# A two-layer attention and MLP kernel: planned instruction order, token-major q and k, a shifted MLP, and row-tiled remainders

## Chip, cores and metric

The kernel runs on one core of one Trainium2 chip. The metric is the device time of one execution in microseconds (us). Engines are called as in the profile: PE is the TensorE, PEld its weight loads, ACT the ScalarE, DVE the VectorE, POOL the GpSimd, SP the SyncE that issues most transfers. A bank is one of the slots of 512 columns that matmuls write to and that the other engines read.

## The reference

Two identical layers on 2048 tokens of width D = 576: windowed attention (32 heads of 18, each token sees the last 256), then an MLP of width 4608.

```python
def A(x, wqkv, wo):                       # H = 32, Dh = 18, W = 256
    q, k, v = split_heads(x @ wqkv)
    s = q @ k.T * Dh ** -0.5              # masked to 0 <= i - j < W
    return merge_heads(softmax(s) @ v) @ wo
def B(x, w1, b1, w2, b2):                 # F = 4608
    return gelu(layernorm(x) @ w1 + b1) @ w2 + b2
for _ in range(2):
    x = x + A(layernorm(x), wqkv, wo)
    x = x + B(layernorm(x), w1, b1, w2, b2)
```

## The kernel before

The tokens go through in chunks of 512 (four tiles of 128), eight chunks over the two layers. 576 is 4 x 128 + 64, so each contraction is five matmuls, the last with 64 rows of zeros. q and k are made head-major, with each head padded from 18 to 32 columns by scattered weights, so that four heads' scores run side by side as 32-row tiles:

```python
def qk_piece(k, g, which, ...):           # 8 groups of 4 heads; 16 pieces per chunk
    for c in range(KD):                   # KD = 5
        e.matmul(bank(bnk)[:, 0:CW], wpad[:, c, g*128:(g+1)*128], xnTa[:, c, :], ...)   # 512 columns
def scores(k, g, u):                      # one unit: writes all four score banks psS
    for (so, qo, nq, col) in parts:
        for j in range(4):
            e.matmul(psS[:, j, col:col+nq*128], kT[32*j:32*j+32, g, s, :], qT[32*j:32*j+32, g, ...],
                     tile_position=(32*j, 0))
    # then two exponentials on ACT (1024 columns each), selects on POOL for the mask
```

A chunk's attention has 8 x 3 such units. The order of instructions is written by hand. While chunk k is in its attention, the MLP of chunk k-1 is run between its parts (`...` marks cuts):

```python
for k in range(NK + 1):
    ...
    G_part(km, 0, ...)              # up projection and gelu, first half, of chunk k-1
    E_part(k, 0, base, byg)         # attention of chunk k, groups 0-3, beside down projection, first half
    G_part(km, 1, ...)              # up projection, second half
    E_part(k, 1, base, byg)         # attention, groups 4-7, beside down projection, second half
    for i in range(CT): att_T(i)    # transposes of the attention output
    ...
    for i in range(CT):             # the tail: nothing but v projections is left to lie beside it
        outproj(k, i, ...); ln_stats(ts[i]); ln_rstd(ts[i], True)
        ... ln_norm_T(ts[i - 1], xnTm, "xm")
```

The next up projection needs all of `xnTm`, so each chunk ends with a chain of output projection, norm and transposes through several engines.

The softmax here doesn't subtract the row's maximum and nothing guards it: scores larger than these inputs give would overflow.

## Time and profile before

| before | value |
|---|---|
| median of its runs beside the changed kernel | 1178.39 us (1175.69 to 1182.75, 4 runs) |
| span of the profiled run, granted clock | 1178.2 us, 0.961 |
| one steady chunk (272.46 to 414.85 us) | 142.39 us, PE busy 128.94 |
| before the first up projection | about 133 us, PE busy 70% of each of its two stages after the projections |

The page's first part gives each engine's busy time, its share of the span and its number of instructions:

```profile
PE 1028.5 (87%) x9312; PEld 580.0 (49%) x9312; DVE 306.8 (26%) x615; ACT 654.1 (56%) x927; POOL 353.2 (30%) x429
```

PE is the bound with 87%, and no other engine comes near. So time can be won in two ways: less work on PE, or fewer of the 150 us in which PE has none. The groups, the chain of waits, the stages and the timeline of before are shown and read in the prediction below.

### The profile page before, as it was taken

The page shows a single profiled execution, that of the slowest core. Times are in us where ns is not written, and L with a number is a line of the kernel's source. Part 1 is how long each engine was busy: PE and PEld are TensorE (multiplying, and loading weights), DVE is VectorE, ACT ScalarE, POOL GpSimd, SP SyncE. Part 2 cuts the span into 40 slices and gives each one's busy share as a digit, 9 for nine tenths or more (in the row PEclk, how much of TensorE's full clock was granted, in tenths as well). Part 3 has the DMA queues.
Part 4 walks back from the last instruction along what each step waited for, and adds up shares of the span by engine and source line. Part 5 has one row for each costly group of instructions (what it writes and reads, how often), then busy time and mean ns, then how long its engine had stood idle before and what let it go on. Part 6 is the DMA issues. An engine that isn't in the chain of part 4 may idle for free.

```text
span 1178.2 us, 22128 instructions
## 1 busy us (share of the span) xinstructions
PE 1028.5 (87%) x9312; PEld 580.0 (49%) x9312; DVE 306.8 (26%) x615; ACT 654.1 (56%) x927; POOL 353.2 (30%) x429
## 2 busy tenths in 40 slices
PE   3677799979999799898999899997998979898798
PEld 1233354544645445455545546454454644545366
DVE  8432312251213412034021521115020240102111
ACT  3364466646657276663656456573756627674432
POOL 9253132330414304151132314143040521424100
PEclk9897899999999899999999999999999989998899
DMA  9501414117230363306332171312633025331640
GB/s 242 155 2 23 85 41 140 54 34 205 70 103 22 71 169 91 101 2 147 92 112 81 29 191 61 112 51 50 199 92 101 17 52 169 93 105 35 179 130 21
DMA packets 158562, 109.78 MB, mean 93 GB/s; under 512 B 74176, under 2 KB 157760, under 8 KB 158464
## 3 DMA queue, kind: packets, MB, share of 16 engines
q1 hardware_dynamic: 151872, 105.41, 32.6%
q0 software_dynamic: 4768, 0.31, 0.8%
q10 hardware_dynamic: 1824, 2.65, 0.6%
q8 instruction: 73, 1.20, 0.4%
q14 instruction: 25, 0.20, 0.1%
HBM read 90.10 MB, written 2.36 MB: 78 GB/s over the span
## 4 chain that ended last, share of the span: by engine, by line
PE 73%; DVE 10%; ACT 8%; issue 5%; POOL 3%; DMA 1%; SPq 0%; POOLq 0%; DVEq 0%
PE ps L479 27%; PE ps L491 21%; PE ps L329 10%; ACT pT L396 5%; PE ps L426 5%; PE ps L388 5%; PE ps L356 4%; DVE st_all L280 3%; DVE x_res L454 3%; POOL pT L407 2%; DVE xn L299 2%; PE ps L464 1%; ACT hT L483 1%; ACT vA L365 1%; DVE mv_all L282 1%
## 5 line engine op out<-in xcount | busy, mean ns | idle before, releaser
L407 POOL TENSOR_SCALAR_AFFINE_SELECT pT<-pT 128x512 bf16<-128x512 bf16 (+1 forms) x368 | 277.4, 776 | 633.2 <-ACT pT L396 622.2
L396 ACT ACTIVATE pT<-ps 128x1024 bf16<-128x1024 f32 (+2 forms) x384 | 351.7, 967 | 168.7 <-PE ps L388 168.5
L479 PE MATMUL ps<-xnTm,w_sb 128*128 128x512 bf16 x1440 | 323.6, 387 | 6.0 <-DMA xnTm<-xn 6.0
L491 PE MATMUL ps<-w_sb,hT 128*128 128x288 bf16 x2304 | 317.5, 290 | 8.7 <-DVE x_res L454 8.1
L483 ACT ACTIVATE hT<-ps,b1col 128x512 bf16<-128x512 f32 x288 | 195.6, 687 | 138.9 <-PE ps L479 138.8
L491 PEld LDWEIGHTS ps<-w_sb,hT 128*128 128x128 bf16 x2304 | 218.6, 99 | 76.7 <-DVE x_res L454 11.3
L479 PEld LDWEIGHTS ps<-xnTm,w_sb 128*128 128x128 bf16 x1440 | 142.8, 100 | 180.8 <-issue 19.8
L454 DVE TENSOR_TENSOR x_res<-ps,x_res 128x576 f32<-128x576 f32 x80 | 60.0, 750 | 370.8 <-PE ps L491 321.9
L426 PE MATMUL ps<-vA,pT 128*128 128x20 bf16 x2880 | 102.8, 172 | 21.1 <-POOL pT L407 20.6
L426 PEld LDWEIGHTS ps<-vA,pT 128*128 128x128 bf16 x2880 | 85.7, 96 | 59.2 <-issue 41.6
L388 PE MATMUL ps<-qT,kT 32*128 32x384 bf16 (+2 forms) x1408 | 74.6, 279 | 37.2 <-ACT pT L396 25.5
L356 PE MATMUL ps<-wv_sb,xnTa 128*128 128x288 bf16 x320 | 58.6, 325 | 49.5 <-ACT vA L365 29.2
L329 PE MATMUL ps<-xnTa,wk_pad 128*128 128x512 bf16 x320 | 86.9, 406 | 16.3 <-DVE kT L335 6.3
L329 PE MATMUL ps<-xnTa,wq_pad 128*128 128x512 bf16 x320 | 84.7, 398 | 5.6 <-DVE kT L335 5.0
L335 DVE CAST qT<-ps 128x512 bf16<-128x512 f32 x49 | 33.8, 690 | 208.6 <-PE ps L329 208.4
L666 POOL TENSOR_TENSOR x_res<-x_res,b2bc 128x576 f32<-128x576 f32 x32 | 44.8, 1400 | 109.5 <-DVE xn L299 109.5
L388 PEld LDWEIGHTS ps<-qT,kT 32*128 32x128 bf16 x1408 | 22.3, 92 | 101.6 <-ACT pT L396 61.5
L356 PEld LDWEIGHTS ps<-wv_sb,xnTa 128*128 128x128 bf16 x320 | 31.5, 108 | 71.3 <-ACT vA L365 37.6
L365 ACT ACTIVATE vA<-ps 128x288 bf16<-128x288 f32 x64 | 26.1, 408 | 65.2 <-PE ps L356 65.2
L335 DVE CAST kT<-ps 128x256 bf16<-128x256 f32 (+1 forms) x78 | 40.4, 541 | 61.7 <-PE ps L329 61.7
L329 PEld LDWEIGHTS ps<-xnTa,wk_pad 128*128 128x128 bf16 x320 | 28.6, 102 | 54.5 <-ACT qT L337 9.4
L286 ACT ACTIVATE lnv<-mv_all 128x1 f32<-128x1 f32 x64 | 12.6, 197 | 68.7 <-DVE mv_all L282 68.7
(35 smaller groups left out, 383.9 us busy)
## 6 DMA issues: line engine op xcount, KB each, us to landing
w_sb<-in_B_w_dram SPq DMA_DIRECT2D x144, 288.0 KB, 4.6
w_sb<-in_B_w_dram SPq DMA_DIRECT2D x72, 512.0 KB, 4.0
w_sb<-in_B_w_dram SPq DMA_DIRECT2D x72, 64.0 KB, 3.8
hT<-in_A_x_dram SPq DMA_DIRECT2D x4, 576.0 KB, 10.8
out_dram<-xn SPq DMA_DIRECT2D x16, 144.0 KB, 1.8
w_sb<-in_A_wqkv_dram ACTq DMA_DIRECT2D x1, 1152.0 KB, 7.7
wv_sb<-in_A_wqkv_dram ACTq DMA_DIRECT2D x1, 576.0 KB, 10.5
wo_sb<-in_A_wo_dram ACTq DMA_DIRECT2D x1, 576.0 KB, 12.7
```

Of the source, the lines that this page charges most:

```text
L329: ins = e.matmul(bank(bnk)[:, 0:CW], wpad[:, c, g * 128:(g + 1) * 128], xnTa[:, c, :], start=(c == 0), stop=(c == KD - 1))
L335: S.add("dve", lambda e: e.tensor_copy(dst, src), reads=[f"pb{bnk}"], writes=wr)
L356: ins = e.matmul(bank(bnk)[:, 0:DHALF], xnTa[:, c, i * 128:(i + 1) * 128], wv_sb[:, c, hh * DHALF:(hh + 1) * DHALF], start=(c == 0), stop= ...
L388: ins = e.matmul(psS[:, j, col:col + nq * 128], kT[32 * j:32 * j + 32, g, s, :], qT[32 * j:32 * j + 32, g, qo * 128:(qo + nq) * 128], star ...
L396: S.add("act", lambda e, h2=h2: e.activation(pT[:, sl, 2 * h2:2 * h2 + 2, lo:hi], psS[:, 2 * h2:2 * h2 + 2, lo:hi], ACT.Exp, scale=SCALE), ...
L407: S.add("pool", lambda e, ap=ap, pat=pat, sgn=sgn, kind=kind: e.affine_select(ap, ap, pattern=pat, compare_op=(ALU.is_ge if kind == "d" el ...
L426: ins = e.matmul(bank(B_O)[:, o:o + VW], pT[:, sl, j, col + qi * 128:col + (qi + 1) * 128], vA[:, sv, 4 * g + j, :], start=(first and n == ...
L454: S.add("dve", lambda e: e.tensor_tensor(dst, src, xr, ALU.add), reads=[f"pb{b0}", f"pb{b0 + stp}", f"x{t}"], writes=[f"x{t}" if outp is N ...
L479: ins = e.matmul(bank(bnk)[:, 0:CW], w1_sb[:, sl, c, fo * 128:(fo + 1) * 128], xnTm[:, c, :], start=(c == 0), stop=(c == KD - 1))
L483: S.add("act", lambda e: e.activation(hT[:, fl, :], bank(bnk)[:, 0:CW], ACT.Gelu_apprx_tanh, bias=b1col[:, f:f + 1]), reads=[f"pb{bnk}", " ...
L491: ins = e.matmul(bank(bb[0] + hh * bb[1])[:, 0:DHALF], hT[:, fl, i * 128:(i + 1) * 128], w2_sb[:, fl, hh * DHALF:(hh + 1) * DHALF], start= ...
L666: S.add("pool", lambda e, t=t: e.tensor_tensor(x_res[:, t, :], x_res[:, t, :], b2bc[:, :], ALU.add), reads=[f"x{t}", "b2"], writes=[f"x{t}"])
```

## The change

Four things are done at once. q and k are computed token-major, unpadded, and brought to the head-major layout by a padded copy and DMA transposes. The two 64-row remainders of a pair of outputs run as two 64-row tiles side by side. The norm's inverse root moves from ACT to POOL. And the instructions are handed to a list scheduler (it places, one after the other, the instruction that can start earliest by the planned costs, the more urgent first), over a shifted order: the second half of a chunk's MLP lies one chunk later, so that a chunk's tail has an up-projection half beside it.

```diff
+    def two_out(lhs, rhs, n, reads, prio, after=()):      # a pair of outputs, q, k, v and output projection
+            for o in range(2):
+                for c in range(4):
+                    ins = e.matmul(bank(bs[o])[:, 0:n], lhs(o, c, full), rhs(o, c, full), start=(c == 0), stop=False)
+                if PAIR and o == 1:
+                    for oo in range(2):
+                        r = slice(64 * oo, 64 * oo + 64)
+                        ins = e.matmul(bank(bs[oo])[:, 0:n], lhs(oo, 4, r), rhs(oo, 4, r), start=False, stop=True,
+                                       tile_position=(64 * oo, 0))
...                                                        # the up projection has the same with 512 columns
+    def qkv(k, i, prio):                                  # one token tile
+        for n, w in enumerate("qkv"):
+            bs = two_out(... xnTa ..., ... wqkv ..., HB, ...)          # HB = 288 columns
...
+                    add("dve", ... e.tensor_copy(qv[:, o * 16:(o + 1) * 16, 0:DH], ...))   # qn, padded to 32 per head
+                add("sp", ... e.dma_start_transpose(dst, qn[:, sl, :]))                    # dst in qT or kT
...
+        add("pool", ... e.tensor_tensor(rstd[...], vtmp[...], nhalf[...], ALU.pow))
...
-    for k in range(NK + 1):                               # G_part, E_part, G_part, E_part, tail by hand
+    for k in range(NK + 1):                               # last number: priority in the list scheduler
+            E(k, range(0, 4), b - 0.5)                    # attention, groups 0-3, of chunk k
+            mm2(k - 2, 1, b)                              # down projection, second half, of chunk k-2
+            G_part(k - 1, 0, b + 1)                       # up projection, first half, of chunk k-1
+            E(k, range(4, 8), b + 1.5)                    # attention, groups 4-7
+            mm2(k - 1, 0, b + 2)                          # down projection, first half, of chunk k-1
+                    qkv(k + 1, i, b + 2.2 + 0.2 * i)
+            tail(k, b + 1.9)
+            G_part(k - 1, 1, b + 3)                       # up projection, second half: beside the tail of chunk k
+    PL.schedule()
```

Below, a cycle is this loop's body; its parts are called first attention half, first up half, second attention half and second up half.

## The prediction

> **What bounds the kernel now.** I read the page first, then the groups of instructions by line, the busy time by stage, the chain that ended last in order of time, and the timeline at single turns of the tensor engine. The page's chain of what ended last is by engine:
> ```profile
> PE 73%; DVE 10%; ACT 8%; issue 5%; POOL 3%; DMA 1%; SPq 0%; POOLq 0%; DVEq 0%
> ```
> So the TensorE (PE) is the bound, and the groups show what it does (busy us, mean ns of one, then idle time before them):
> ```profile
> L396 ACT ACTIVATE pT<-ps 128x1024 bf16<-128x1024 f32 (+2 forms) x384 | 351.7, 967 | 168.7 <-PE ps L388 168.5
> L479 PE MATMUL ps<-xnTm,w_sb 128*128 128x512 bf16 x1440 | 323.6, 387 | 6.0 <-DMA xnTm<-xn 6.0
> L491 PE MATMUL ps<-w_sb,hT 128*128 128x288 bf16 x2304 | 317.5, 290 | 8.7 <-DVE x_res L454 8.1
> L329 PE MATMUL ps<-xnTa,wk_pad 128*128 128x512 bf16 x320 | 86.9, 406 | 16.3 <-DVE kT L335 6.3
> L329 PE MATMUL ps<-xnTa,wq_pad 128*128 128x512 bf16 x320 | 84.7, 398 | 5.6 <-DVE kT L335 5.0
> L356 PE MATMUL ps<-wv_sb,xnTa 128*128 128x288 bf16 x320 | 58.6, 325 | 49.5 <-ACT vA L365 29.2
> ```
> The means there are latencies; matmuls overlap. The spacing comes from undisturbed blocks of the chain (start us, us):
> ```profile
> 1137.87 19.43 PE ps L479 x90
> 1157.30 17.65 PE ps L491 x144
> ```
> One 512-column matmul takes 19.43/90 = 0.216 us, one of 288 columns 17.65/144 = 0.1225 us. The stages are in the busy time by stretch (from:to, length, then PE, PEld, DVE, ACT, POOL busy, clock, DMA):
> ```profile
> 17.40:51.00 33.60, 27.70 (x120) 12.84 (x120) 22.35 (x50) 8.33 (x19) 14.28 (x21) 0.90 0.89 174
> 51.00:104.40 53.40, 37.53 (x488) 17.44 (x488) 17.77 (x40) 37.08 (x55) 28.24 (x40) 0.90 0.07 14
> 104.40:132.60 28.20, 19.82 (x93) 9.82 (x90) 10.59 (x22) 5.64 (x18) 5.59 (x4) 0.68 0.23 47
> 272.46:414.85 142.39, 128.94 (x1206) 73.00 (x1204) 37.34 (x74) 83.17 (x114) 42.42 (x52) 0.96 0.35 95
> 1097.70:1178.20 80.50, 77.21 (x468) 46.33 (x468) 6.06 (x8) 28.58 (x39) 0.00 (x0) 0.96 0.35 112
> ```
> They are: projections of chunk 0; attention of chunk 0, with no MLP beside it; its tail (output projection, norm, transposes); a steady chunk; the last MLP. A steady chunk has PE at 129 of 142 us, no other engine above 83. The first 133 us are slack, some of it at a clock of 0.68.
>
> Last, what a turn into row tiling and back costs. Timeline (start us, us):
> ```profile
> 157.30 2.38 PE L491 MATMUL ps<-w_sb,hT 128*128 128x288 bf16 x18
> 159.61 0.40 PE L388 MATMUL ps<-qT,kT 32*128 32x256 bf16 x8
> 159.94 0.56 PE L426 MATMUL ps<-vA,pT 128*128 128x20 bf16 x16
> ```
> The 18 full matmuls should take 18 x 0.1225 = 2.205 us, but the row-tiled scores start only after 2.31: 0.10 lost going in. The eight scores are two sets of four side by side, 2 x 256 columns, 2 x 0.11 = 0.22 us of streaming; the next full matmul starts after 0.33: 0.11 lost coming out. **One excursion costs about 0.2 us**, though none of these instructions shows a wait.
>
> **What the Trainium skill says.** "TensorEngine Tiling (Array Packing)", Tiling Modes, Key Properties: changing the tiling mode drains the TensorE, while tiles of one mode run in parallel. The trace agrees with both: 0.2 us per round trip above, and four scores taking the time of one. "TensorE: Matmul & The Clock Gate", Part 1: back-to-back matmuls are N/2.4 ns + about 2.5 ns apart (215.7 ns at 512); the trace has 216. Same part: the clock is halved until the engine has been busy for a window of about 3.4 us; the trace agrees in kind, with clock 0.68 in the gappy tail of chunk 0 against 0.96 to 1.0 in steady stretches. So filling gaps pays twice.
>
> **The change part by part**, in PE time.
> 1. q and k token-major. Before, heads padded from 18 to 32 columns make 640 matmuls of 512 columns, 640 x 0.216 = 138.2 us, and v has 320 x 0.1225 = 39.2: 177.4 us. Unpaired and token-major, q, k and v are 32 token tiles x 3 x 2 halves x 5 = 960 matmuls of 288: 117.6 us. **Saves 60 us.** It adds 64 DMA transposes of 128x1024, and moves v's 64 evictions (26.1 us) from ACT to DVE, which gets 192 of 288 columns, by ACT's 408 ns about 78 us, for the 74 us of q and k evictions it had: DVE about even, ACT 26 down.
> 2. Row-tiled remainders. A pair of outputs takes nine slots, not ten, plus an excursion. MLP up: 8 chunks x 18 pairs = 144, each -0.216 + 0.2 = -0.016 us: 2 saved. Projections: 96 for q, k, v and 32 for the output, each -0.1225 + 0.2 = +0.08: 10 lost. **Costs 8 us net**; streaming falls by 47 us but 272 excursions cost 54. I believe the turn costs the same with 64-row tiles as with 32-row ones; this is the least secure step.
> 3. Norm by POOL pow instead of Ln and Exp on ACT: 12.6 + 13.0 us off ACT, off the bound. It shortens a chain in the tail only if POOL isn't busy.
> 4. The shifted, list-scheduled order. The second half of the down projection of one chunk goes beside the attention of the chunk after next, so that the tail of each chunk and the transposes lie beside an up-projection half (90 matmuls, 19.4 us). This takes waits away, and is best summed by stage.
>
> One cycle's PE work after: up projection 36 pairs/2 = 18 x (9 x 0.216 + 0.2) = 38.6; down 288 x 0.1225 = 35.3; q, k, v 12 x (9 x 0.1225 + 0.2) = 15.6; output projection 4 x 1.3 = 5.2; scores 24 units x (0.22 + 0.2) = 10.1; PV 384 matmuls, which the timeline spaces by about 0.025 us (16 in 0.40), 9.6. Sum 114.4. Before by the same rates it is 38.9 + 35.3 + 22.2 + 4.9 + 10.1 + 9.6 = 121, against 140 measured (six steady chunks, 838 us): **19 us per chunk of waits and clock**. I expect 6 of these to stay, a judgement: the timeline shows PE waiting 0.5 to 0.9 us for ACT at each change between up projection and attention, four a cycle, and with three banks for projections and down projection some eviction waits can't be filled.
>
> By stage: first matmul at 14 (before 17.5: no scatter of padded weights, but the same load, norm and transpose). Projections of chunk 0: 12 x (1.3 + 0.6 waiting for one of three banks) = 23. Attention of chunk 0: bound by its exponentials, ACT busy 37 before, so 42 (before 53). First attention half of chunk 1 beside chunk 0's tail: 12 units x 1.95 of ACT, 25. Rest of chunk 1: 19.3 + 19.7 + 17.6 + 15.6 + 5.2 + 19.3 = 97, less about 10 done early in the ACT-bound stretch: 87. Six cycles: 6 x 114.4 - 5 (first chunk of layer 2 has three quarters of the blocks) - 15.6 (the last has no next projections) = 666, plus 6 x 6 waits = 702. End: three down halves of 17.65, two up halves of 19.3, and 4 to the output = 95.5, with 3 of waits 98. Sum 14 + 23 + 42 + 25 + 87 + 702 + 98 = 991; half clock in the opening gaps, an estimate from the 0.90 and 0.68 above, adds 14: **1005 us**, a ratio of 0.853. So of 174 us gained some 52 are arithmetic (parts 1 and 2) and some 120 are gaps.
>
> **Rivals.** (a) The 64-row turn is free: 54 us less, 951. For: the authors chose it. Against: the excursions above. (b) The transposes become the wait. Their issue is serial on one queue:
> ```profile
> 250.07 5.19 SPq L446 DMA_TRANSPOSE attT<-attq  x4
> ```
> That is 1.3 us for 640 columns, so an estimated 2.1 for 1024. After the attention of a chunk come 4 + 4 x 1.3 and 8 x 2.1 = 27 us before the next scores (q and k have one buffer). Against: 19.3 of up projection and some 10 to 20 of projections stand there to cover it. If 10 us per cycle stick out: 1075. (c) The fixed order is made from planned costs; where real ones differ (the excursions, issue on one queue) engines stand before a blocked instruction, and the 19 us per chunk return: 6 x 13 more, 1085. (d) ACT becomes the bound: 654 - 26 - 26 - 13 for q and k = 589 us, 59% of 1005, but near PE in attention halves (12 x 1.95 = 23 against 27). It doesn't bind except in chunks 0 and 1.
>
> **Range and chances.** (a) partly true gives 960 to 980, (b) or (c) partly 1040 to 1065: range 955 to 1065. To be within 2% all the gaps must stay and part 1 must be lost to transposes: 3%. Slower by over 2%: 1%.
>
> **What would show it.** Steady cycle near 120 us with PE near full; 288-column matmuls replacing L329; each 64-row pair starting 0.1 us late and its follower 0.1 us late, with no wait named; PE's idle time (span less busy, 150 us before) under 90; clock over 0.96. Wrong, if 64-row turns show no extra spacing, if scores wait for transposes of q or k in every cycle, or if the cycle stays over 130.

## The result

The changed kernel took 1046.28 us (median of 4 runs, 1041.77 to 1053.11) beside 1178.39. Ratios are the mean time of one kernel's fast runs over that of the other's of the same rounds, so not quite the ratio of the medians; here 0.8881, with a 95% interval of 0.8822 to 0.8939. The time lies in the range, 41 us above its centre. The profiled run has a span of 1046.7 us and a clock of 0.933, lower than before.

The page after, first part and chain by engine:

```profile
PE 954.4 (91%) x9312; PEld 537.5 (51%) x9312; DVE 331.3 (32%) x840; ACT 576.3 (55%) x705; POOL 380.8 (36%) x517
```

```profile
PE 75%; POOL 10%; issue 8%; ACT 3%; DMA 2%; DVE 2%; POOLq 0%; SPq 0%
```

PE has 74 us less to do and idles for 1046.7 - 954.4 = 92 us, not 150. POOL's share of the chain went from 3 to 10%, a first hint of where the rest is. The groups of matmuls after (busy us, mean ns, idle before and its releaser):

```profile
L680 PE MATMUL ps<-xnTm,w_sb 128*128 128x512 bf16 x1152 | 290.4, 394 | 6.4 <-ACT pT L563 6.4
L683 PE MATMUL ps<-xnTm,w_sb 64*128 64x512 bf16 x288 | 57.1, 394 | 0.0
L716 PE MATMUL ps<-w_sb,hT 128*128 128x288 bf16 x2304 | 312.7, 286 | 0.0
...
L485 PE MATMUL ps<-wqkv,xnTa 128*128 128x288 bf16 x768 | 129.2, 306 | 26.0 <-DMA xnTa<-xn 25.9
```

The 640 padded matmuls of 512 columns are gone; for q, k and v there are now 768 full ones of 288 columns and, on a line not shown, 192 of 64 rows. L683 is the 64-row pair of the up projection; no wait is named ahead of it. What it costs shows in the timeline of one stretch of up projection (start us, us):

```profile
164.78 1.90 PE L680 MATMUL ps<-xnTm,w_sb 128*128 128x512 bf16 x8
166.61 0.39 PE L683 MATMUL ps<-xnTm,w_sb 64*128 64x512 bf16 x2
166.93 1.90 PE L680 MATMUL ps<-xnTm,w_sb 128*128 128x512 bf16 x8
```

Eight full matmuls should take 8 x 0.216 = 1.73 us, but the pair starts after 1.83: 0.10 lost going in. The pair streams 0.216, but the next full one starts after 0.32: 0.10 lost coming out. In the raw starts of the trace the loss is 96 ns in and 103 ns out. A pair of 512 columns so takes 415 ns in place of 2 x 216 = 432, and one of 288 columns 321 ns in place of 245.

The busy time by stretch (from:to, length, then PE, PEld, DVE, ACT, POOL busy, clock, DMA):

```profile
16.78:35.54 18.76, 16.24 (x90) 8.04 (x91) 12.19 (x38) 0.00 (x0) 8.72 (x16) 0.91 1.32 188
35.54:103.92 68.38, 42.15 (x566) 23.96 (x567) 26.64 (x72) 36.29 (x48) 31.25 (x44) 0.72 0.48 113
103.92:147.50 43.58, 32.10 (x397) 17.80 (x398) 26.22 (x63) 22.55 (x24) 26.67 (x34) 0.77 0.29 57
...
589.80:712.00 122.20, 119.26 (x1206) 67.14 (x1205) 40.71 (x104) 74.42 (x88) 45.96 (x62) 0.96 0.48 117
...
832.90:953.20 120.30, 106.16 (x1087) 58.48 (x1085) 22.89 (x61) 74.48 (x90) 45.82 (x61) 0.89 0.39 108
```

The first three are the projections of chunk 0, its attention, and its tail beside the first attention half of chunk 1. The fourth is a full cycle: PE is busy 98% of it, in 122 us where a chunk took 142. The fifth is the last cycle: it has 119 PE instructions less than the one above and 13 us less PE work, yet takes almost as long. So the new time is lost in the opening and in the last cycle, and both have a low clock.

Against the prediction's stages, by bounds taken from the first up projection and from ACT's table loads:

| stage | predicted, us | measured, us |
|---|---|---|
| to the first matmul | 14 | 16.8 |
| projections of chunk 0 | 23 | 18.8 |
| attention of chunk 0 | 42 | 68.4 |
| chunk 0's tail beside the first half of chunk 1 | 25 | 43.6 |
| half clock in the opening | 14 | inside the lines above |
| rest of chunk 1 (to 234.9) | 87 | 87.4 |
| five cycles (to 832.9) | 5 x 120.4 - 5 = 597 | 598.0 |
| last cycle (to 953.2) | 120.4 - 15.6 = 104.8 | 120.3 |
| end | 98 | 93.5 |
| sum | 1005 | 1046.8 |

The opening is 29.5 us over, the last cycle 15.5, the end 4.5 under, the rest within 1.5.

### The profile page after: what moved, and what is told of

The parts are those of the page before. It is cut to its first block, busy times and chain, and to the rows that moved or that the text cites. A ratio compares the mean times of both kernels' runs of the same rounds, so it can differ in the third digit from the quotient of the medians.

```text
span 1046.7 us, 22452 instructions
## 1 busy us (share of the span) xinstructions
PE 954.4 (91%) x9312; PEld 537.5 (51%) x9312; DVE 331.3 (32%) x840; ACT 576.3 (55%) x705; POOL 380.8 (36%) x517
## 4 chain that ended last, share of the span: by engine, by line
PE 75%; POOL 10%; issue 8%; ACT 3%; DMA 2%; DVE 2%; POOLq 0%; SPq 0%
PE ps L716 27%; PE ps L680 27%; POOL pT L584 9%; PE ps L485 6%; PE ps L601 5%; PE ps L683 5%; PE ps L554 4%; ACT pT L563 3%; PE ps L489 1%; DMA xnTa<-xn 1%; DVE st_all L413 1%; DMA hT<-in_A_x_dram 1%; POOL rstd L426 0%; DMA qT<-qn 0%; POOL x_res L659 0%
## 5 line engine op out<-in xcount | busy, mean ns | idle before, releaser
L680 PE MATMUL ps<-xnTm,w_sb 128*128 128x512 bf16 x1152 | 290.4, 394 | 6.4 <-ACT pT L563 6.4
L680 PEld LDWEIGHTS ps<-xnTm,w_sb 128*128 128x128 bf16 x1152 | 102.1, 100 | 141.1 <-issue 35.4
L635 DVE TENSOR_TENSOR x_res<-ps,x_res 128x288 f32<-128x288 f32 x160 | 71.0, 452 | 317.3 <-PE ps L716 263.2
L485 PE MATMUL ps<-wqkv,xnTa 128*128 128x288 bf16 x768 | 129.2, 306 | 26.0 <-DMA xnTa<-xn 25.9
L485 PEld LDWEIGHTS ps<-wqkv,xnTa 128*128 128x128 bf16 x768 | 68.4, 102 | 58.8 <-issue 24.5
L521 DVE CAST qn<-ps 128x288 bf16<-128x288 f32 x128 | 52.7, 453 | 95.7 <-PE ps L489 95.7
L611 DVE RECIPROCAL rinv<-ps 128x16 f32<-128x16 f32 x64 | 16.4, 256 | 167.0 <-PE ps L601 167.0
L683 PE MATMUL ps<-xnTm,w_sb 64*128 64x512 bf16 x288 | 57.1, 394 | 0.0
L436 DVE TENSOR_SCALAR xn<-x_res,mv_all,rstd 128x576 bf16<-128x576 f32 x60 | 43.9, 732 | 22.9 <-POOL rstd L426 9.0
L683 PEld LDWEIGHTS ps<-xnTm,w_sb 64*128 64x128 bf16 x288 | 13.8, 93 | 63.5 <-issue 63.5
L413 DVE BATCH_NORM_STATS2 st_all<-x_res 128x6 f32<-128x288 f32 x96 | 41.4, 452 | 1.1
```

The source lines that it names most:

```text
L413: add("dve", lambda e, i=i, s=s: e.bn_stats(st_all[:, t, i, :], s[:, t, i * HB:(i + 1) * HB]), reads=res, writes=[f"st{t}_{i}"], cost=0.43 ...
L485: ins = e.matmul(bank(bs[o])[:, 0:n], lhs(o, c, full), rhs(o, c, full), start=(c == 0), stop=False)
L521: add("dve", lambda e, o=o, b=bs[o], qv=qv: e.tensor_copy(qv[:, o * 16:(o + 1) * 16, 0:DH], bank(b)[:, 0:HB].rearrange("p (h d) -> p h d", ...
L635: add("dve", lambda e: e.tensor_tensor(x_res[:, t, sl], bank(b)[:, 0:HB], x_res[:, t, sl], ALU.add), reads=[b], writes=[f"x{t}h{hh}"], cos ...
L680: ins = e.matmul(bank(bks[o])[:, 0:n], w1_sb[:, sl, col:col + 128], xnTm[:, k % 2, c, 0:n], start=(c == 0), stop=False)
L683: ins = e.matmul(bank(bks[oo])[:, 0:n], w1_sb[64 * oo:64 * oo + 64, sl, 2048 + pp * 128:2048 + (pp + 1) * 128], xnTm[64 * oo:64 * oo + 64, ...
```

## The experiments

Four kernels went to the chip in each of three batches, each with its own runs of the kernel before beside it (medians 1177.78, 1177.75 and 1178.67 us). The theory was that the turns into row tiling cost about what the tiling saves, that the shift and the plan give most of the gain, and that the opening's loss comes from scores and exponentials taking turns. The rivals were that turns are cheap, that transposes set the pace, and that the arithmetic of q and k gives the gain.

### after_again: the changed kernel unchanged

> The changed kernel as it is, timed once more beside its variants on one chip. Every theory: 1040 to 1053 us, as in its first four runs; it is the measure for the three runs beside it.

Measured: 1046.58 us (1042.74 to 1051.07), ratio 0.8887 [0.8859, 0.8914]. This is the value that the others are held against.

### e_nopair and e_pair_mlp: no pairs, and pairs in the up projection alone, with a new plan

```diff
-PAIR = True
-W1W = 2304
+PP = False      # projections
+PM = False      # up projection; True in e_pair_mlp, where W1W stays 2304
+W1W = 2560
 ...             # each use of PAIR becomes PP or PM; unpaired remainders are zero-padded to 128 rows
```

> No row-tiled pairs anywhere: remainder padded with zeros to 128 rows, as before the change. Turn theory (each pair loses 96 ns going in and about 103 ns coming out, read from the spacing in the changed kernel's trace): up projection 144 x (432 - 415) = +2.4 us, projections 128 x (245 - 321) = -9.8 us, so about 7 us faster than the changed kernel. Rival (a pair is worth the matmul that it saves): streaming grows by 144 x 0.216 + 128 x 0.1225 = 47 us, so 40 us or more slower.

Measured: 1034.12 us (1032.56 to 1036.31), ratio 0.8783 [0.8758, 0.8808].

> Pairs kept in the up projection alone; q, k, v and output projection padded. Turn theory: -9.8 us against the changed kernel, and 2 us under the kernel without any pair. Rival: 128 x 0.1225 = 16 us slower than the changed kernel.

Measured: 1047.38 us (1045.30 to 1051.23), ratio 0.8900 [0.8872, 0.8927].

Without pairs the kernel is 12 us faster, so they bring nothing here. But the two runs don't fit one theory: the pairs of the up projection should save 2 us and seem to cost 13. The scheduler makes a new plan for each set of costs, and the plans differ: in e_nopair the first up projection starts at 140.7 us, in the changed kernel at 148.2 by ACT's table load. So what was measured was partly the plan. The next two hold it fixed.

### e_plan_nopair and e_plan_mlp_full: the same plan, with the 64-row pairs replaced

```diff
                 if PAIR and o == 1:
                     for oo in range(2):
-                        r = slice(64 * oo, 64 * oo + 64)
-                        ins = e.matmul(bank(bs[oo])[:, 0:n], lhs(oo, 4, r), rhs(oo, 4, r), start=False, stop=True, tile_position=(64 * oo, 0))
+                        ins = e.matmul(bank(bs[oo])[:, 0:n], lhs(oo, 4, full), rhs(oo, 4, full), start=False, stop=True)
 ...             # planned costs unchanged; rows 64 to 127 of the last weight block are zeroed
```

In e_plan_mlp_full this is done in the up projection alone. The order of PE's instructions was compared and is the same as in the changed kernel. Not all else is: e_plan_nopair also drops four small weight loads at the start and adds three memsets.

> The changed kernel's plan kept to the letter (same tasks, same order on the tensor engine, same waits, same banks); only the two row-tiled matmuls of each pair are two full matmuls with zero-padded weights. This takes out what a new plan does. Turn theory: 144 x (432 - 415) = +2.4 us in the up projection and 128 x (245 - 321) = -9.8 us in the projections, so 5 to 10 us faster than the changed kernel (1036 to 1041). Rival (a pair saves what its streaming says): 35 to 47 us slower.

Measured: 1042.43 us (1036.39 to 1046.12), ratio 0.8845 [0.8813, 0.8877].

> Same plan again, pairs kept in the q, k, v and output projections, two full matmuls in their place in the up projection alone. Turn theory: the pair of 512 columns costs 96 + 216 + 103 = 415 ns against 432, so 0 to 3 us slower than the changed kernel, and 7 to 12 us slower than the run without any pair. The run of the pairs in the up projection alone (1047) asks whether a pair there costs some 10 us that the spacing doesn't show; if so, this run is 10 us faster than the changed kernel.

Measured: 1045.26 us (1041.74 to 1046.89), ratio 0.8877 [0.8850, 0.8904].

e_plan_nopair's timeline of the same kind of stretch (start us, us):

```profile
161.34 1.89 PE L682 MATMUL ps<-xnTm,w_sb 128*128 128x512 bf16 x8
163.07 0.59 PE L686 MATMUL ps<-xnTm,w_sb 128*128 128x512 bf16 x2
163.50 1.89 PE L682 MATMUL ps<-xnTm,w_sb 128*128 128x512 bf16 x8
```

Ten full matmuls take 163.50 - 161.34 = 2.16 us, and eight and a pair took 166.93 - 164.78 = 2.15. The first two lines show no loss between them: 1.73 us for eight. So in the up projection the pair is worth nothing. Taken from the spacings, all pairs save 144 x 17 ns = 2.4 us there and cost 128 x 76 ns = 9.7 us in the projections, 7.3 net. The whole-kernel times give 1046.6 x (0.8845/0.8887 - 1) = -4.9 us and -1.2 us; their intervals overlap with that of the changed kernel, so the sign of either isn't settled by them. Of the 4.9 us, 3.5 lie before the first up projection (144.7 us by ACT's table load, against 148.2), where the dropped loads may have a part. The rival, under which replacing the pairs would cost 47 us, is refuted.

### e_spread and e_spread2: spread the down projection over an attention half

```diff
+        if pace is not None:
+            order.add(pace)                               # in the list scheduler: not before this score unit
 ...
-            mm2(k - 2, 1, b)
+            mm2(k - 2, 1, b, [] if last else SC[-12:])    # pieces of 6 matmuls paced by the 12 score units
 ...                                                       # e_spread2: mm2(k - 1, 0, ...) too, the second half
```

> In the first attention half of each chunk, each group of six down-projection matmuls may only be placed once a matching score unit has been placed (two groups per unit, three groups ahead), so that the filler lasts to the end of the half. My theory of the attention halves: one unit can't be shorter than 2.44 us (scores, then two exponentials, one set of score banks), and the list scheduler puts 18 matmuls in each of the first eight units (3.04 us each) and none in the last four (about 2.5 us with the tensor engine idle); spread evenly 12 units take about 31 us where the half took 36, so about 5 us per chunk for six chunks: 25 to 30 us faster, idle time and half clock at the ends of the halves gone. Rival (the half is bound by the exponentials or by the select anyway): no change, within 5 us.

Measured: 1035.38 us (1032.96 to 1036.63), ratio 0.8788 [0.8764, 0.8813].

> The down projection paced by the score units in both attention halves. The run that paced the first half alone gained 11 us, not 25 to 30: its trace shows that I had the wrong half, the first is already full with the next chunk's projections, and the idle stretches at half clock (seen at 190 to 205, 313 to 330, 443 to 450 us) end the second halves, which have 36 us for 27 us of work. Theory: second halves go from 36 to about 31.5 us, seven of them, so 25 to 34 us below the changed kernel beyond the 11: 1003 to 1012. Rival (the exponentials and the select set the length of the half): 1035, as with the first half alone.

Measured: 1041.02 us (1039.08 to 1044.95), ratio 0.8838 [0.8811, 0.8865].

e_spread gains 11 us. e_spread2's 6 us aren't settled, as its interval overlaps with the changed kernel's. Both are far from what was expected. The stretches show why: first a second attention half, then the first one of the next cycle, of the changed kernel, then the same two of e_spread2.

```profile
291.40:327.70 36.30, 33.72 (x450) 22.09 (x448) 9.10 (x22) 24.54 (x25) 17.23 (x22) 0.92 0.35 94
357.10:392.80 35.70, 35.36 (x479) 23.69 (x478) 17.93 (x43) 24.51 (x26) 19.50 (x25) 1.00 0.47 117
```

```profile
286.30:321.90 35.60, 35.51 (x482) 24.14 (x480) 11.55 (x28) 24.50 (x26) 17.23 (x23) 1.00 0.21 45
350.30:388.40 38.10, 34.26 (x442) 22.83 (x443) 13.06 (x34) 24.58 (x26) 18.20 (x24) 0.87 0.55 140
```

The PE hole and the low clock moved from one half to the other. The filler, that is the work that can lie between the score units (down projection, projections, output projection), is short over the cycle as a whole: filling one half empties the other. By ACT's table loads e_spread2's cycles from 228.3 us are 121.9 and 123.2 us long, no shorter than the changed kernel's 122.2 and 120.9; its last one is, with 114.1 against 120.3. I had also named the wrong half for e_spread, for first halves were full already. My expectation of 25 us and more fell.

### e_open: weight loads after the transposes of the opening

```diff
-        w1_load(0, [f"q{n0 - 1}"])
-    w2_load(0, 0, [f"q{n0 - 1}"])
+        w1_load(0, [f"q{n0 - 1}"] + [f"xa{i}" for i in range(n0)])
+    w2_load(0, 0, [f"q{n0 - 1}"] + [f"xa{i}" for i in range(n0)])
```

> One thing changed in the opening: the 17 weight loads of the first MLP are issued after the four transposes of chunk 1's normed input, not before. Theory: in the changed kernel these loads stand ahead on the one issuing queue, the transposes land at 53, and the tensor engine, whose next instruction needs them, is idle from 46 to 53 us; so 6 to 9 us faster (1037 to 1041), all of it before 60 us. Rival (attention of chunk 0 is paced by its exponentials, and the hole is made up by 148 us): under 2 us.

Measured: 1044.58 us (1040.69 to 1046.27), ratio 0.8861 [0.8834, 0.8888]. The timeline of the changed kernel and then of e_open, at the start of chunk 1's projections (in brackets the idle time before and its releaser; SPq is the transfer queue's issue):

```profile
39.47 6.32 SPq L365 DMA_DIRECT2D w_sb<-in_B_w_dram  x9
...
45.90 7.34 SPq L445 DMA_TRANSPOSE xnTa<-xn  x4
...
52.90 1.14 PE L485 MATMUL ps<-wqkv,xnTa 128*128 128x288 bf16 x4 [6.95 <-DMA xnTa<-xn]
```

```profile
47.19 1.14 PE L485 MATMUL ps<-wqkv,xnTa 128*128 128x288 bf16 x4 [0.89 <-DMA xnTa<-xn]
```

The transposes stood behind weight loads in one queue, and the hole of 7 us on PE was theirs; ordered otherwise, it is gone. Yet the first up projection starts 2.8 us earlier only (145.4 against 148.2), and the total moves by about 3 us, within the intervals: later transposes of k then stand behind the weights. A hole at one place of a loose stretch is worth little.

### e_split: the scores of a unit as two halves, in the opening alone

```diff
+        cut = k == 0 or (k == 1 and g < 4)
+        for js in (((0, 1), (2, 3)) if cut else ((0, 1, 2, 3),)):
 ...
-        add("pe", fn, reads=rd, writes=[f"pb{j}" for j in range(4)], cost=0.06 + ncol * 0.00053, prio=prio, lat=0.15)
+            sc = add("pe", fn, reads=rd, writes=[f"pb{j}" for j in js], cost=0.06 + ncol * 0.00053, prio=prio, lat=0.15)
```

The first half of a unit's scores then needs only the two banks that the first exponential has read.

> In the attention stretches of the opening alone (chunk 0, first half of chunk 1: 36 units) the scores of a unit are two tasks of two heads each, so the next unit's first pair may run while the second exponential of this unit reads the other banks. Theory for the 44 us by which the opening missed my prediction: I took the exponentials' busy time as the pace, but one set of score banks makes each unit wait for scores and exponentials in turn (2.44 us where the exponentials take 1.94); so up to 36 x 0.5 = 18 us, 8 to 18 us faster, all before the first up projection, which starts near 135 and not 148. Rival (the pace of the opening is the select on POOL with the bias adds and transposes, or issue order): under 4 us.

Measured: 1033.35 us (1030.25 to 1034.22), ratio 0.8767 [0.8745, 0.8788], clock 0.944 to 0.950. The timeline of the changed kernel where PE has nothing else, then of e_split:

```profile
192.43 0.40 PE L554 MATMUL ps<-qT,kT 32*128 32x384 bf16 x8
192.88 1.94 ACT L563 ACTIVATE pT<-ps 128x1024 bf16<-128x1024 f32 x2 [0.51 <-PE ps L554]
194.88 0.40 PE L554 MATMUL ps<-qT,kT 32*128 32x256 bf16 x8
195.32 1.94 ACT L563 ACTIVATE pT<-ps 128x1024 bf16<-128x1024 f32 x2 [0.50 <-PE ps L554]
```

```profile
77.32 4.48 ACT L565 ACTIVATE pT<-ps 128x1024 bf16<-128x1024 f32 x6 [0.88 <-PE ps L558]
```

In the changed kernel all four score banks are written by one unit, so the next scores wait for both exponentials, and these for the scores: a unit takes 195.32 - 192.88 = 2.44 us, not the 1.94 of its exponentials. In the opening the changed kernel has the same gap, 0.5 to 0.7 us ahead of each unit's exponentials from 80 to 98 us. In e_split six exponentials follow each other without a gap. Attention of chunk 0 in e_split, by stretch:

```profile
34.00:93.10 59.10, 48.13 (x575) 25.87 (x573) 27.15 (x76) 36.28 (x48) 31.05 (x44) 0.79 0.58 132
```

It fell from 68.4 to 59.1 us, the first up projection starts at 133.6 us, and the kernel gains 13 us, inside what was expected. The plan is new here too, but the hole behind the weight loads is still there (5.25 us before 52.20), so the gain isn't that. This mechanism is confirmed.

### e_head: undo the token-major q and k alone

```diff
-    wqkv = sb("wqkv", [P, KD, 3 * D], BF16)
+    wv_sb = sb("wv_sb", [P, KD, D], BF16)
+    wq_pad = sb("wq_pad", [P, KD, G * 128], BF16)
+    wk_pad = sb("wk_pad", [P, KD, G * 128], BF16)
 ...
+    def qk(k, g, prio):                                   # 5 matmuls of 512 columns, as in the kernel before
+        for which, wpad in (("q", wq_pad), ("k", wk_pad)):
 ...                                                       # no qn, no transposes of q and k; shift, pairs and scheduler stay
```

> Undoes the token-major q and k alone: padded head-major projections (640 matmuls of 512 columns, straight into the tiles that the scores read, no transposes of q and k), v and everything else as in the changed kernel, planned anew. My step 1: 640 x 0.216 = 138.2 us against 64 pairs of outputs x 1.32 = 84.5 us as the trace shows them with their turns: 54 us more work on the bound, so 40 to 60 us slower than the changed kernel (1087 to 1107). Rival (the 64 transposes and their waits give most of the saving back): within 20 us of the changed kernel, under 1067.

Measured: 1054.56 us, ratio 0.8949 [0.8928, 0.8970] from three fast runs of 1053.7 to 1055.2; the fourth, the profiled one, took 5200.82 us (see the last section), so its profile can't be read for time. Only 8 us were lost where 40 to 60 were expected. So most of the PE work saved by part 1 of the change lay beside idle time, or was given back by the casts and transposes that came with it, or by the clock; without a usable trace these aren't told apart. And 8 us is no more than a new plan alone can move (7 us between e_nopair and e_plan_nopair, by their ratios). One thing is visible in the fast runs: their clock is 0.972 against 0.933. With one core busy the clock is either half or full, as the Trainium skill has it in "TensorE: Matmul & The Clock Gate", Part 1, and the trace agrees: the changed kernel's clock records are 0.5 or 1.0 only, and those at 0.5 add up to 139.9 us. Time at half clock is then 2 x (1 - clock) x span: an estimate of 59 us here and 140 us in the changed kernel. With more work on PE, less of its time is at half clock.

### e_unshift: undo the shift alone

```diff
     for k in range(NK + 1):
+            G_part(k - 1, 0, b)
-            E(k, range(0, 4), b - 0.5)
-            mm2(k - 2, 1, b)
-            G_part(k - 1, 0, b + 1)
-            E(k, range(4, 8), b + 1.5)
-            mm2(k - 1, 0, b + 2)
+            E(k, range(0, 4), b + 0.5)
+            mm2(k - 1, 0, b + 1)
+            G_part(k - 1, 1, b + 2)
+            E(k, range(4, 8), b + 2.5)
+            mm2(k - 1, 1, b + 3)
 ...
-            G_part(k - 1, 1, b + 3)
```

This is the order of the kernel before, with everything else of the change.

> Undoes the shift alone: as before the change, the first down half goes beside the first attention half, the second up half follows, the second down half goes beside the second attention half, and the tail of the chunk has no up half beside it. Still list-scheduled, token-major, paired. My step 4: the tail (transpose, output projection, norm, transpose, 12 to 17 us of latency by the traces of both kernels) is exposed again save for what q, k, v of the next chunk fill: 6 to 12 us per chunk, seven chunks, so 40 to 80 us slower (1087 to 1127). Rival (the list scheduler alone removes the gaps): within 15 us of the changed kernel.

Measured: 1185.59 us (1184.63 to 1187.11), ratio 1.0068 [1.0044, 1.0092]: 139 us slower than the changed kernel, far over the 40 to 80 expected, and 0.7% slower than the kernel before. The stretches of two tails, and one line of the list of waits (us in total, times, longest):

```profile
241.60:270.50 28.90, 14.86 (x87) 7.55 (x89) 17.55 (x44) 1.23 (x1) 10.68 (x14) 0.62 0.66 112
384.90:410.00 25.10, 12.58 (x76) 6.30 (x76) 15.72 (x39) 0.58 (x1) 10.03 (x13) 0.64 0.66 118
```

```profile
PE ps L485 <- DMA xnTa<-xn: 80.7, 9, 17.0
```

Each tail stands bare for 25 to 29 us with PE half busy and the clock at 0.62 to 0.64, and PE waits 81 us for transposes of the next chunk's input, 17.0 of them at the start (the changed kernel waits 25.9, 16.8 of them at the start). The first up projection starts at 100.6 us, not 148.2, but mainly because chunk 1's first attention half now comes after it: PE idles 42.6 us before it, against 57.0 in the changed kernel. And a cycle takes 143 us, not 121. So the whole gain of this kernel hangs on the shift: take it out and nothing is left. But the parts work together. In this order transposes of the new q and k (at 242.26 and 249.95 us) fall into the bare tail, so e_unshift charges to the shift a cost that part 1 brought. It isn't shown that the shift alone, in the kernel before, would give as much, for the tail of before has no q and k transposes in it; that kernel was not built.

### e_best: what helped, together

```diff
+PP = False      # no pairs, as e_nopair
+PM = False
 ...             # and the edits of e_spread, e_open and e_split
```

> The four edits that gained or that I think gain, together: no pairs, down projection paced in the first half, the opening's transposes ahead of the weights, split scores in the opening. If the gains add: 12 + 11 + 3 + 8 to 18, so 1003 to 1013. If the halves short of filler are what is left, the first two overlap: about 1020.

Measured: 1015.23 us (1013.62 to 1016.94), ratio 0.8618 [0.8597, 0.8638], clock 0.955 to 0.960, correct, between the two expectations. It beats both kernels, the changed one by 3%. Its last cycle shows what spreading does. Its first attention half, with the down projection spread, and its second one, not spread:

```profile
807.40:837.60 30.20, 27.36 (x397) 19.42 (x397) 5.80 (x14) 24.54 (x25) 17.18 (x22) 1.00 0.28 87
...
858.00:893.10 35.10, 27.75 (x396) 18.86 (x396) 5.81 (x14) 24.52 (x26) 17.19 (x22) 0.86 0.25 82
```

Both have the same work. Spread, it takes 30.2 us at full clock, about 12 units of 2.44 us and a table load; not spread, 35.1. There the scheduler places the down projection at the start, where it delays the scores to one unit in about 3 us, and has none left for the end, where PE waits at half clock.

## Why the prediction was right or wrong

**The range and the direction held, and the cycles held best.** Five cycles and the rest of chunk 1 came out within 1.5 us of the sums. PE's time in them is bound by its own work, as in the stage sums, and a sum of measured spacings is good there. The terms held too: split as in the table below, the cycle from 589.80 us has about 113 us of streaming and turns, where the prediction has 114.4, and about 9 of waits and half clock, where it has 6. That the total lies in the range is partly luck: its upper part stood there for rivals (b) and (c), and the missing 41 us came from neither.

**The step on the turn's cost held.** The prediction's least secure step was that a turn costs the same with 64-row tiles as with 32-row ones. It measured 96 + 103 ns, where 200 was taken. With it the "8 net" of part 2 stands at 7.3 by spacings, and rival (a), 951 us, is out: the pairs bring nothing.

**The first step that failed is "Attention of chunk 0: bound by its exponentials, ACT busy 37 before, so 42", and with it the 25 us of the half after.** I took the busy time of ACT for its pace. The kernel before showed 53.4 us in the same place, which I put down to slack. In fact scores and exponentials share one set of banks and take turns, 2.44 us a unit where 1.94 was taken; e_split removes this and gains 13 us. For 36 units in the opening the gap is 36 x 0.5 = 18 us at most, an estimate from full units. Another 7 us is the hole behind the weight loads, which e_open removes, though most of that comes back. What is left of the 29.5 us I put down to the clock of 0.72 to 0.77, the tail's latency and POOL, whose selects and bias additions share one queue there; no run separates these, and this stays open.

**The second is "15.6 (the last has no next projections)".** I took work off the last cycle as if PE bound it. It has less work and is as long as the others (120.3 us), because its attention halves are bound by the taking of turns, and the plan spends its filler early. The two halves show it, 34.8 us with PE busy 27.7 and 27.8, and e_best's 30.2 against 35.1 us confirms it.

```profile
832.90:867.70 34.80, 27.68 (x393) 18.45 (x391) 5.81 (x14) 24.56 (x26) 17.54 (x23) 0.86 0.42 121
...
890.40:925.20 34.80, 27.78 (x394) 18.51 (x392) 5.81 (x14) 24.55 (x27) 17.23 (x22) 0.86 0.25 78
```

**The step "some 52 are arithmetic (parts 1 and 2) and some 120 are gaps" is right as a count and wrong as a cause.** I split each interval between starts of successive matmuls into nominal spacing, 95 ns where the tile shape changes, excess at half clock up to one more spacing, and waiting:

| PE's time, us | before | after | difference |
|---|---|---|---|
| streaming at nominal spacing | 924 | 819 | -105 (predicted -60 and -47) |
| turns between tile shapes | 36 | 84 | +48 (predicted +54) |
| half clock | 36 | 34 | -2 |
| waits | 157 | 84 | -73 |

So 57 of the 132 us are arithmetic, near the 52. But e_head, which gives part 1's streaming back, loses 8 us, not 54 or 60. Where the rest went stays open; half clock can't be all of it, as it costs the changed kernel 34 us in the table. And e_unshift, which keeps parts 1 to 3, has no gain at all. What the gain hangs on is the tails hidden by the shift; with the shift in place, part 1 is worth 8 us. The waits fell by 73, not 120: the missing 47 are about the 29.5 and 15.5 us by which the opening and the last cycle missed their sums.

**Rivals (b), (c) and (d).** Transposes of q and k (b) don't hold up the steady cycles: a full cycle has PE busy 119.3 of 122.2 us. The estimate of 2.1 us to issue one was too high: two in a row took 2.62 to 2.70 us of the queue between 441 and 471 us. In e_unshift PE does wait for transposes, those of the normed input, where nothing covers them. The planned order (c) shows as a time that a new plan alone moves by some 7 us (e_nopair against e_plan_nopair, though a few loads and small copies differ too), perhaps by 15 (e_pair_mlp is 13 us slower than e_nopair, where the spacings say 2 faster), and as filler spent early, not as a loss in every cycle. ACT (d) binds in the opening and the last cycle, through turns with PE, at 55% busy overall. Part 3 of the change, the inverse root on POOL, was undone in no run, so what it is worth isn't shown.

**The tests named for the profile.** The cycle near 120, the 288-column matmuls and the 0.1 us on either side of each pair came true. Idle PE time "under 90" was 92. "Clock over 0.96" was wrong: 0.933, as the opening and the last cycle run at half clock in part.

## What to carry to other kernels

Time a stage that isn't bound by one engine from the loop that its buffers make (here scores, exponentials, scores: 2.44 us), not from the busy time of its busiest engine. Ask of each saved matmul whether its stretch waits for PE at all; here undoing the order that puts work beside the tails cost 139 us, and undoing the largest saving of matmuls 8. When a scheduler plans the order, hold the plan fixed to measure an edit, since a new plan alone moved this kernel by about 7 us.

## What the Trainium skill lacked or had wrong

- "TensorEngine Tiling (Array Packing)", Tiling Modes, Key Properties says that changing the tiling mode drains the TensorE, but gives no cost. Here a turn cost 96 ns going from full to 64-row tiles and 103 ns coming back, and about 200 ns there and back for 32-row tiles.
- The same page's Overview, Theoretical Speedup, gives up to 2x for a dimension of 64 or less. Two 64-row matmuls among full ones took 415 ns at 512 columns, where two full ones take 432 (1.04x), and 321 at 288 columns, where two full ones take 245 (0.76x). The page doesn't set the turns against the gain.
- "TensorE: Matmul & The Clock Gate", Part 1, knows a half and a full clock, a peak-current state with three cores busy, and in its caveats a quarter that was seen to stick for 50 us and more. One execution of e_head took 5200.82 us: its 512-column matmuls were 1.278 us apart in the median, from start to end, against 0.216, a sixth of the speed, while its exponentials took 967 ns on average, as in the kernel before. It came once in all the runs of this case, and no page has this state.
